# Four decay rows per head: picked by matmuls and a PSUM copy in place of eight small DMAs

## The chip, the cores and the metric

The kernel runs on one core of one Trainium2 chip. The metric is the device time of one execution in microseconds, as the median of several runs. TensorE (PE) multiplies, with its weight loads listed apart as PEld; VectorE (DVE), ScalarE (ACT) and GpSimd (POOL) do the elementwise work; SyncE (SP) and ScalarE issue the DMAs of this program. The kernel is written with tiles taken from pools; a scheduler orders the instructions of each engine when the program is built, and each engine runs its own list strictly in that order.

## The reference, cut to what matters

Causal attention with a decay term over four batches of eight heads (sequence 576, head size 64), then two dense layers of the same shape (512 to 2048 to 512) over the 2304 tokens:

```python
scores = (q @ k.T) / 8
cum    = cumsum(log(clip(f, 1e-4, 1)))
scores = where(causal, -1e9, scores + cum[:, None] - cum[None, :])
x      = softmax(scores) @ v                      # heads side by side: 2304 x 512
x      = relu(x @ w_in) ** 2 @ w_out              # first dense layer
out    = elu(x @ w_in2) @ w_out2                  # second dense layer
```

## The kernel before, in words

The decay is put into the score matmul. Below the 64 rows of transposed q and k, four more rows hold 8·cum and -8·cum, each as a rounded part and its remainder, against rows of ones. The contraction then runs over 68 rows and gives score plus decay in one product. All 32 heads' rows for their first 256 positions are made by `split_c` in the tile `ca`: head on the partition, the four rows along the free axis (4 x 512). A head needs them turned, as four partitions (64 to 67) of its operand tile `rawA`.

Batch 0 is handled in a special way. Its first 256 rows (kind "A", eight heads) come first, since they feed the first unit of the first dense layer; the rest of its rows (kinds "4" and "B") and the other batches follow. For kind "A", `fetch_plain` loads two heads into one `rawA` tile: rows 0 to 63 from `in_first_dram` and the values from `in_firstv_dram` on the SP queue, and the four decay rows from `ca` by one DMA per head, issued on ScalarE (the `nc.scalar.dma_start` of line 277).

While attention of batch 0 runs, the weights of the first dense layer are decoded. They come as 16 half tiles (`wraw`, `raws_w`), five of them fetched at the start. For each one ScalarE takes an absolute value (L153 in `words`), DVE does four steps (L154 to L157), ScalarE rounds to the high part `w` (L173), and GpSimd subtracts (L135) for the low part. The working tile of these steps is `wt`, with the pool tag `"o"` of pool `xa`, which has two buffers. The first five half tiles' decoding is spread over the first steps (`W_AT`). TensorE fills gaps with matmuls on a zero tile (`busy`, L250, tile `idle`): 60 at the start and a few per step.

Names in the rows: `s` scores in PSUM, `ea` the exponentials of kind "A", reduced by DVE (L354) and exponentiated by ScalarE (L357); `pt` their transposes, `pv` the product with the values, `xA` its copy, `pr` the turned row sums; `eb`, `pp` the same for kind "B"; `ph`, `o`, `pH`, `O`, `P` the dense layers. PSUM tiles `pt`, `pr` come from a pool of three banks (`ps_t`).

Of the kernel before, what the change touches and what calls it, by code (L numbers as in the profile page):

```python
# [10 lines left out]
F32 = mybir.dt.float32  # L11
F32R = mybir.dt.float32r
I32 = mybir.dt.int32
AF = mybir.ActivationFunctionType
ALU = mybir.AluOpType

B, H, S, D = 4, 8, 576, 64
# [25 lines left out]
PLAIN = (0,)  # L43
# [29 lines left out]
def f32(ap):  # L73
    return ap.bitcast(F32)
# [10 lines left out]
def attention_then_moe_kernel(ctx, tc, first, firstv, plain, qkv, aug0, f, w1, w2, out):  # L85
    nc = tc.nc
    PS = bass.MemoryType.PSUM

    def pool(stack, name, bufs, side, **kw):
        return stack.enter_context(tc.tile_pool(name=name, bufs=bufs, side=side, reuse_waits="tile", **kw))  # L90
# [5 lines left out]
    xa = pool(ctx, "xa", 2, "left")  # L96
# [27 lines left out]
    def copy(eng, dst, x, scale=None):  # L124
        if eng == "a":
            nc.scalar.activation(out=dst, in_=x, func=AF.Copy, scale=1.0 if scale is None else scale)  # L126
        elif eng == "p":
            nc.gpsimd.tensor_scalar(dst, x, 1.0 if scale is None else scale, 0.0, op0=ALU.mult, op1=ALU.add)
        elif scale is None:
            nc.vector.tensor_copy(dst, x)  # L130
        else:
            nc.vector.tensor_scalar(dst, x, scale, None, op0=ALU.mult)
# [65 lines left out]
    ps_t = pool(at, "ps_t", PSB[1], "right", space=PS)  # L198
# [14 lines left out]
    e4s = [a1.tile([128, 640], F32, name=f"e4_{s}") for s in range(2)]  # L213
    me = getattr(nc, MEM)
    ca = wa.tile([B * H, 4, 512], F32R, tag="w7", name="ca")
    me.memset(f32(ca), 1.0)
    nc.gpsimd.memset(mz, 0.0)
    mask(mz[:, 384:512], [[-1, 128]])
# [37 lines left out]
    pairs = {}  # L256
# [9 lines left out]
    def fetch_plain(b, h, part):  # L266
        g = b * H + h
        k = h % 2
        if part == "A":
            if k == 0:  # L270
                if h // 2 < BUFS["raw"]:
                    t = ab.tile([128, ALL], F32, tag="raw", name="rawA", bufs=BUFS["raw"])
                else:
                    t = hd.tile([128, RAW], F32, tag="qk1", name="rawA", bufs=BUFS["qs"])
                nc.sync.dma_start(out=t[0:64, 0:1024], in_=first[h // 2])
                for i in range(2):
                    nc.scalar.dma_start(out=t[64:68, 512 * i:512 * i + 512], in_=f32(ca[g + i:g + i + 1]))
                nc.sync.dma_start(out=t[:, 1024:1280], in_=firstv[h // 2])
                pairs[b, h // 2] = t
            t = pairs[b, h // 2]  # L280
            raws[b, h, part] = Plain(t, 512 * k - Q0, 512 * k + 256, t[:, 1024 + 128 * k:1152 + 128 * k].rearrange("p (j d) -> p j d", d=D))
            return
        if k == 0:
            t = ab.tile([128, ALL], F32, tag="raw", name="rawB", bufs=BUFS["raw"])
        else:
            t = hd.tile([128, RAW], F32, tag="qk1", name="rawC", bufs=BUFS["qs"])
        nc.sync.dma_start(out=t[0:64, 0:RAW], in_=plain[h])
        nc.sync.dma_start(out=t[64:68, 0:RAW], in_=aug[g])
        if k == 0:
            v = t[:, RAW:ALL]  # L290
        else:
            v = hd.tile([128, 5 * D], F32, tag="vv", name="vp", bufs=BUFS["vv"])
        nc.sync.dma_start(out=v, in_=qkv[b, h, :, RAW:ALL])
        raws[b, h, part] = Plain(t, 0, QW, v.rearrange("p (j d) -> p j d", d=D))

    def aug_split():
        cp, cn = (ab.tile([32, 2, S - 256], F32R, tag="eb", name=t, bufs=BUFS["eb"]) for t in ("cp", "cn"))
        split_c(cp, cn, slice(256, S))
        return cp, cn
# [53 lines left out]
    def reduce_min(e, s, m, nm, init=BIG):  # L353
        nc.vector.tensor_tensor_reduce(out=e, in0=s, in1=m, scale=-0.125, scalar=init, op0=ALU.add, op1=ALU.min, accum_out=nm)  # L354
# [15 lines left out]
    def soft_a(b, h, hh):  # L370
        e = ab.tile([128, 384], F32, tag="ea", name="ea", bufs=BUFS["ea"])
        nm = ab.tile([128, 2], F32, tag="nm2", name="nm2", bufs=3)
        z = sums("A", b, h // 2, h % 2)
        s = ps_s.tile([128, 512], F32, tag="s", name="s")
        scores(s[:, 0:256], hh, Q0 + 128, 0, 256, True, True)
        scores(s[:, 256:512], hh, Q0, 0, 256, True, True)
        parts = [slice(0, 256), slice(256, 384)]
        for i, c in enumerate(parts):
            n = c.stop - c.start
            reduce_min(e[:, c], s[:, c], mz[:, 512 - n:512], nm[:, i:i + 1])  # L380
            expo(e[:, c], nm[:, i:i + 1], z[:, i:i + 1])
        return e
# [156 lines left out]

    def soft(b, hp, kind, k):  # L540
        if kind == "A":
            es[b, hp, kind, k] = soft_a(b, 2 * hp + k, heads[b, hp, k])
            yield
        elif kind == "B":
            es[b, hp, kind, k] = yield from soft_b(b, 2 * hp + k, heads[b, hp, k])
        else:
            e4[b, hp] = soft_4(b, hp, [heads[b, hp, i] for i in range(2)])
            yield
# [180 lines left out]
    for i in range(len(todo) + LAG):  # L729
# [16 lines left out]
        if i < len(todo):  # L746
            sg = soft(*todo[i])
            b, hp, kind, k = todo[i]
        else:
            sg = iter(())  # L750
        if i >= LAG:
            o = todo[i - LAG]
            og = outs(*o)
        else:
            o, og = None, iter(())
# [416 lines left out]
```

## Time and profile before

| what | us |
|---|---|
| three timed runs | 1035.57, 1040.85, 1042.72 |
| their median | 1040.85 |
| the profiled execution, its own time | 1037.57 |
| span from its first to its last instruction | 1035.7 |
| TensorE busy in it | 1020.5 (99%) |
| VectorE busy in it | 683.1 (66%) |
| ScalarE busy in it | 547.4 (53%) |
| GpSimd busy in it | 275.0 (27%) |

Busy shares are averages over stages with different limits, so the table alone does not tell what bounds a stage. The mean granted TensorE clock of the whole execution is 0.994 of full speed.

### The profile page before, as it was taken

Reading aid. Unit: us, or ns where it says so; the run is one execution under the profiler, and the core shown is the slowest. Engines: PE = TensorE matmul, PEld = TensorE weight load, DVE = VectorE, ACT = ScalarE, POOL = GpSimd, SP = SyncE. Lnnn points to the kernel's source line nnn. Section 1 sums busy time; section 2 is a strip of 40 time slices with the busy share of each in tenths; the row PEclk is TensorE's granted clock in tenths of the full one; section 3 lists DMA queues with packets and bytes.
Section 4 is the critical chain, followed back from the end, with each engine's and each line's share of the span. In section 5 each row is a group of like instructions: output and inputs, shape, how many; then the busy total and the mean of one; then the engine's idle time right before and its main releaser. Section 6 shows DMA issues by size and latency. Waiting matters only on the chain.

```text
span 1035.7 us, 17605 instructions
## 1 busy us (share of the span) xinstructions
PE 1020.5 (99%) x6391; PEld 903.5 (87%) x6391; DVE 683.1 (66%) x1543; ACT 547.4 (53%) x1218; POOL 275.0 (27%) x296
## 2 busy tenths in 40 slices
PE   8999999999999999999999999999999999999998
PEld 7676798999999998889988888988988998899897
DVE  4995467665675638847385868896555989754554
ACT  3875688777786734524253535463344565433331
POOL 3565587675776210004103040300000000000000
PEclk8999999999999999999999999999999999999999
DMA  8853645554551164433454555544314465443502
GB/s 247 227 156 109 203 140 170 191 171 145 153 164 54 45 222 137 141 123 143 135 171 170 196 204 199 216 139 179 123 61 158 149 223 170 136 169 124 156 21 82
DMA packets 73881, 158.46 MB, mean 153 GB/s; under 512 B 9316, under 2 KB 34660, under 8 KB 73764
## 3 DMA queue, kind: packets, MB, share of 16 engines
q1 hardware_dynamic: 73732, 157.29, 46.4%
q8 instruction: 50, 0.82, 0.3%
q14 instruction: 35, 0.29, 0.1%
q10 hardware_dynamic: 64, 0.07, 0.0%
HBM read 115.15 MB, written 39.22 MB: 149 GB/s over the span
## 4 chain that ended last, share of the span: by engine, by line
PE 81%; DVE 9%; DMA 3%; POOL 2%; ACT 2%; issue 2%; POOLq 0%; ACTq 0%; DVEq 0%; SPq 0%
PE O L186 29%; PE P L186 16%; PE pH L186 11%; PE o L186 6%; PE ph L186 5%; PE pt L418 4%; PE pv L425 3%; PE s L350 2%; DVE wt L156 2%; PE s L351 2%; PE s L346 1%; DMA x<-yl 1%; PE pv L422 1%; DVE wt L157 1%; POOL qk L135 1%
## 5 line engine op out<-in xcount | busy, mean ns | idle before, releaser
L186 PEld LDWEIGHTS P<-xu,v 128*128 128x128 f32 x1536 | 200.5, 189 | 10.7 <-ACT hs L1013 0.6
L186 PE MATMUL P<-xu,v 128*128 128x256 f32 x1536 | 203.7, 282 | 0.5 <-ACT hs L1013 0.5
L186 PE MATMUL O<-v,gh 128*128 128x512 f32 x576 | 169.2, 393 | 1.4 <-ACT gh L984 1.4
L186 PE MATMUL pH<-xu,w 128*128 128x512 f32 (+1 forms) x672 | 140.8, 360 | 0.0
L186 PEld LDWEIGHTS pH<-xu,w 128*128 128x128 f32 x672 | 114.0, 188 | 20.2
L186 PE MATMUL O<-gh,w 128*128 128x512 f32 (+1 forms) x448 | 122.6, 362 | 0.0
L186 PEld LDWEIGHTS O<-v,gh 128*128 128x128 f32 x576 | 102.8, 188 | 19.4 <-ACT gh L984 1.8
L186 PE MATMUL O<-v,gl 128*128 128x512 f32 x288 | 101.0, 393 | 0.0
L186 PEld LDWEIGHTS O<-gh,w 128*128 128x128 f32 x448 | 79.8, 189 | 14.1
L135 POOL TENSOR_TENSOR yl<-pr,yh 128x512 fp32r<-128x512 f32 x18 | 25.2, 1398 | 249.9 <-ACT yh L833 172.1
L1013 ACT ACTIVATE hs<-P 128x256 f32<-128x256 f32 x128 | 48.0, 381 | 79.5 <-PE P L186 78.8
L135 POOL TENSOR_TENSOR qk<-raw,qk 64x704 fp32r<-64x704 f32 (+1 forms) x48 | 75.7, 1578 | 21.0 <-ACT qk L126 15.7
L186 PE MATMUL O<-gl,w 128*128 128x512 f32 (+1 forms) x224 | 80.1, 363 | 0.0
L1016 DVE TENSOR_TENSOR hs<-P,hs 128x256 f32<-128x256 f32 x96 | 40.4, 422 | 57.9 <-PE P L186 56.0
L186 PE MATMUL o<-gh,w 128*128 128x256 f32 x384 | 75.3, 290 | 0.0
L1038 ACT ACTIVATE g<-g 128x512 f32<-128x512 f32 x64 | 40.2, 629 | 54.8 <-DVE g L1030 32.9
L186 PE MATMUL ph<-xu,w 128*128 128x256 f32 x480 | 67.5, 287 | 1.0 <-DMA xu<-x 0.8
L153 ACT ACTIVATE wt<-wraw 128x512 f32<-128x512 f32 x57 | 38.2, 671 | 55.8 <-DMA wraw<-in_w_dram 42.0
L587 ACT ACTIVATE gh<-g 128x512 fp32r<-128x512 f32 (+1 forms) x80 | 46.9, 586 | 39.3 <-DVE g L586 34.8
L984 ACT ACTIVATE gh<-g 128x512 fp32r<-128x512 f32 x72 | 45.4, 631 | 35.4 <-DVE g L1039 28.6
L586 DVE TENSOR_TENSOR g<-g 128x512 f32<-128x512 f32 (+1 forms) x56 | 45.4, 811 | 26.9 <-ACT g L582 26.7
L186 PEld LDWEIGHTS ph<-xu,w 128*128 128x128 f32 x480 | 60.8, 190 | 1.6 <-DMA xu<-x 1.1
(153 smaller groups left out, 2089.1 us busy)
## 6 DMA issues: line engine op xcount, KB each, us to landing
xu<-x SPq DMA_DIRECT2D x66, 512.0 KB
wraw<-in_w_dram SPq DMA_DIRECT2D x57, 512.0 KB
raw<-in_qkv_dram SPq DMA_DIRECT2D x24, 800.0 KB
x<-yh SPq DMA_DIRECT2D x31, 256.0 KB
x<-yl SPq DMA_DIRECT2D x31, 256.0 KB
x<-xs SPq DMA_DIRECT2D x16, 320.0 KB
xu<-x SPq DMA_DIRECT2D x16, 256.0 KB
raws_w<-in_w_dram SPq DMA_DIRECT2D x7, 512.0 KB
```

What stands on the lines that cost most here:

```text
L135: nc.gpsimd.tensor_tensor(out=dst, in0=x, in1=f32(hi), op=ALU.subtract)
L153: nc.scalar.activation(out=f32(t), in_=f32(hi), func=AF.Abs)
L156: nc.vector.scalar_tensor_tensor(t, hi, -0x40000000, t, op0=ALU.bitwise_and, op1=ALU.bitwise_or)
L186: nc.tensor.matmul(out=dst, lhsT=l, rhs=r, start=first and i == 0, stop=last and i == n - 1, skip_group_check=skip)
L418: seen[0] = nc.tensor.transpose(dst, src, ident[:, c0:c0 + 128])
L425: seen[0] = nc.tensor.matmul(out=dst, lhsT=hh[2][:, J, :], rhs=hl[i], start=first and i == 0, stop=last and i == 1)
L586: (nc.vector if sq == "v" else nc.gpsimd).tensor_tensor(out=g[:, 0:n], in0=g[:, 0:n], in1=g[:, 0:n], op=ALU.mult)
L587: nc.scalar.activation(out=gh[:, 0:n], in_=g[:, 0:n], func=AF.Copy)
L984: nc.scalar.activation(out=gh, in_=g, func=AF.Copy)
L1013: nc.scalar.activation(out=o, in_=x, func=AF.Copy)
L1016: nc.vector.tensor_tensor(o, y, x, op=ALU.add)
L1038: nc.scalar.activation(out=gs[i], in_=gs[i], func=AF.Exp)
```

## The change

Line 277's eight DMAs go away. In their place `pick_rows(h)` multiplies `ca` with a matrix that holds a single one. The tile `one` (32 x 160, zero but for a one at column 67 + 4p of partition p) is made once by GpSimd; a 128-column window of it, starting at column 4h + 3 - r, moves row r of head h to output partition 64 + r. Four such matmuls of 512 columns accumulate in one PSUM bank `pk`, and partitions 64 to 67 of it are copied to `rawA`, by VectorE for even heads and by ScalarE for odd ones. Heads 0 and 1 are picked before the scores of head 0, head h + 1 before those of head h. `one` is allocated under the tag `"o"`.

```diff
+    one = xa.tile([B * H, 160], F32R, tag="o", name="one")
+    nc.gpsimd.memset(f32(one), 0.0)
+    nc.gpsimd.affine_select(out=one, in_=f32(one), pattern=[[1, 160]], compare_op=ALU.not_equal, fill=1.0, base=-67, channel_multiplier=-4)
     me.memset(f32(ca), 1.0)
...
                 nc.sync.dma_start(out=t[0:64, 0:1024], in_=first[h // 2])
-                for i in range(2):
-                    nc.scalar.dma_start(out=t[64:68, 512 * i:512 * i + 512], in_=f32(ca[g + i:g + i + 1]))
                 nc.sync.dma_start(out=t[:, 1024:1280], in_=firstv[h // 2])
...
+    def pick_rows(h):
+
+        t, k = pairs[0, h // 2], h % 2
+        pk = ps_t.tile([128, 512], F32, tag="t", name="pk")
+        for r in range(4):
+            c = 4 * h + 3 - r
+            nc.tensor.matmul(out=pk, lhsT=one[:, c:c + 128], rhs=ca[:, r, :], start=r == 0, stop=r == 3)
+        copy("va"[k], t[64:68, 512 * k:512 * k + 512], pk[64:68, :])
...
         if kind == "A":
+            if b in PLAIN:
+                h = 2 * hp + k
+                for i in ([0, 1] if h == 0 else [h + 1] if h < H - 1 else []):
+                    pick_rows(i)
             es[b, hp, kind, k] = soft_a(b, 2 * hp + k, heads[b, hp, k])
```

The scheduler makes new lists from this. The lists differ in the work of batch 0 and agree after it. The text below speaks of three places in them. The first is ScalarE's list at the last two of the first six decay DMAs; `ea` and `zA` are the exponentials of a head and their sums. Before:

```order
L277 DMA rawA<-ca 4x1x512 [waits DMAHW2_49]
L277 DMA rawA<-ca 4x1x512 [waits DMAHW4_49]
L153 ACTIVATE wt<-raws_w 128x512 [waits DMAHW7_49]
L357 ACTIVATE ea,zA<-ea,nm_266 128x256 [waits DVE_49]
L357 ACTIVATE ea,zA<-ea,nm_266 128x128 [waits DVE_49]
L153 ACTIVATE wt<-raws_w 128x512
L277 DMA rawA<-ca 4x1x512 [waits DMAHW6_49]
```

ScalarE's list at the same place after the change (`pk` is the PSUM bank of a head's picked rows, `w_0` the first decoded weight tile):

```order
L228 ACTIVATE nm_149<-fr 32x1 [waits Activation_49]
L153 ACTIVATE wt<-raws_w 128x512 [waits DMAHW7_49]
L173 ACTIVATE w_0_254<-wt 128x512 [waits DVE_49]
L126 ACTIVATE rawA<-pk 4x512 [waits PE_49]
L153 ACTIVATE wt<-raws_w 128x512 [waits DMAHW0_49,Pool_49]
L369 ACTIVATE ea,zA<-ea,nm_277 128x256 [waits DVE_49]
```

The first half tile's absolute value now follows the logarithm's table work directly, where six DMA issues with waits stood, and the second half tile's has got a wait for GpSimd that it did not have.

The second place is VectorE's list where the first half tiles are decoded; before, behind the reduction of the second head's scores (`nm_289` is its minimum):

```order
L354 ISA ea,nm_289<-s,mz 128x128
L354 ISA nm_289 128x1
L154 TENSOR_SCALAR wt<-wt 128x512 [waits Activation_49]
L155 TENSOR_SCALAR wt<-wt 128x512 [waits DVE_49]
L156 SCALAR_TENSOR_TENSOR wt<-raws_w,wt 128x512 [waits DMAHW7_49,DVE_49]
L154 TENSOR_SCALAR wt<-wt 128x512 [waits Activation_49]
L157 SCALAR_TENSOR_TENSOR wt<-raws_w,wt 128x512 [waits DVE_49]
```

VectorE's list there after the change, where `cn` is the last of the split decay rows:

```order
L237 SCALAR_TENSOR_TENSOR cn<-cum,cn 32x320 [waits DVE_49]
L154 TENSOR_SCALAR wt<-wt 128x512 [waits Activation_49]
L155 TENSOR_SCALAR wt<-wt 128x512 [waits DVE_49]
L156 SCALAR_TENSOR_TENSOR wt<-raws_w,wt 128x512 [waits DMAHW7_49,DVE_49]
L157 SCALAR_TENSOR_TENSOR wt<-raws_w,wt 128x512 [waits DVE_49]
L130 COPY rawA<-pk 4x512 [waits PE_49] x2
L366 ISA ea,nm_277<-s,mz 128x256 [waits PE_49,Pool_49]
```

The whole decoding of the first half tile has moved ahead of the first two heads' reductions, and ahead of the copies of heads 0 and 2. Before, the second half tile's L154 ran between the first one's L156 and L157; now the four steps of each of the first five half tiles end before the next one's begin.

The third place is TensorE's list behind the filling matmuls of the start; before:

```order
L250 MATMUL idle<-zero 128x256 x59
L346 MATMUL s<-rawA 128x256 [waits DMAHW2_49,DMAHW1_49]
L346 MATMUL s<-rawA 128x256
L250 MATMUL idle<-zero 128x256 x3
L346 MATMUL s<-rawA 128x256 [waits DMAHW4_49]
```

TensorE's list there after the change, from the last eight of twelve picking matmuls (heads 0, 1 and 2) on, which follow the fillers:

```order
L305 MATMUL pk<-ca,one 128x512 x8
L358 MATMUL s<-rawA 128x256 [waits DMAHW1_49,DVE_49]
L358 MATMUL s<-rawA 128x256
L255 MATMUL idle<-zero 128x256 x3
L358 MATMUL s<-rawA 128x256 [waits Activation_49]
```

Picking matmuls have come between the fillers and the first scores, and head 0's scores wait for VectorE's copy, head 1's for ScalarE's, where both waited for decay DMAs.

## Rows read from the trace of the kernel before

**Rows 1.** Stretches: start:end, length; busy us of each engine (instructions); clock, DMA share, GB/s.

```profile
14.00:18.00 4.00, 4.00 (x14) 3.37 (x14) 2.25 (x11) 3.08 (x10) 0.06 (x1) 0.50 0.84 259
18.00:22.00 4.00, 4.00 (x15) 3.01 (x13) 2.49 (x6) 0.49 (x1) 1.37 (x2) 0.50 0.95 247
...
26.00:50.00 24.00, 22.71 (x129) 16.48 (x128) 23.41 (x61) 19.90 (x54) 14.47 (x15) 1.00 0.82 229
...
700.00:800.00 100.00, 100.00 (x620) 89.68 (x620) 52.56 (x102) 38.87 (x81) 0.00 (x0) 1.00 0.37 128
```

**Rows 2.** The critical chain, 7 to 27 us: start, length, what held it.

```profile
7.46 4.97 DMA rawA<-ca
...
12.56 1.37 PE s L346 x4
```

**Rows 3.** Who waited for whom, 9 to 27 us: total, times, longest.

```profile
ACT wt L153 <- DMA rawA<-ca: 8.8, 1, 8.8
DVE ea L354 <- PE s L346: 7.5, 2, 5.9
PE s L346 <- DMA rawA<-ca: 1.7, 1, 1.7
```

**Rows 4.** Timeline to 15 us: issues on SP and ACT, the first half tile.

```profile
10.83 0.55 SPq L731 DMA_DIRECT2D aug<-in_aug_dram  x1
...
14.45 0.66 ACT L153 ACTIVATE wt<-raws_w 128x512 f32<-128x512 f32 x1 [8.77 <-DMA rawA<-ca]
```

**Rows 5.** VectorE's timeline: the last decoding step of half tiles 1, 2 and 5.

```profile
18.75 0.68 DVE L157 SCALAR_TENSOR_TENSOR wt<-raws_w,wt 128x512 int32<-128x512 int32 x1
...
24.22 0.84 DVE L157 SCALAR_TENSOR_TENSOR wt<-raws_w,wt 128x512 int32<-128x512 int32 x1
...
36.59 0.69 DVE L157 SCALAR_TENSOR_TENSOR wt<-wraw,wt 128x512 int32<-128x512 int32 x1
```

**Rows 6.** Groups by line and shape, 10 to 90 us: busy, mean ns, idle before.

```profile
L135 POOL TENSOR_TENSOR w<-wt,w 128x512 fp32r<-128x512 f32 x16 | 21.5, 1344 | 20.5 <-ACT w L173 20.5
...
L173 ACT ACTIVATE w<-wt 128x512 fp32r<-128x512 f32 x16 | 10.1, 629 | 8.7 <-DVE wt L157 8.6
...
L153 ACT ACTIVATE wt<-wraw 128x512 f32<-128x512 f32 x9 | 6.1, 673 | 1.2 <-POOL w L135 1.1
...
L126 ACT ACTIVATE ea<-pt 128x384 f32<-128x384 f32 x8 | 3.9, 484 | 4.0 <-PE pt L418 3.9
...
L126 ACT ACTIVATE xA<-pv 64x256 f32<-64x256 f32 x8 | 3.0, 375 | 1.0 <-POOL x L135 0.5 <-PE pv L422 0.4
```

**Rows 7.** Timeline: a decoding on VectorE, free and beside GpSimd; copies from PSUM.

```profile
16.88 0.42 DVE L154 TENSOR_SCALAR wt<-wt 128x512 f32<-128x512 f32 x1
17.34 0.43 DVE L155 TENSOR_SCALAR wt<-wt 128x512 int32<-128x512 int32 x1
17.80 0.69 DVE L156 SCALAR_TENSOR_TENSOR wt<-raws_w,wt 128x512 int32<-128x512 int32 x1
...
30.59 1.47 POOL L135 TENSOR_TENSOR w<-wt,w 128x512 fp32r<-128x512 f32 x1
...
30.95 1.66 DVE L156 SCALAR_TENSOR_TENSOR wt<-wraw,wt 128x512 int32<-128x512 int32 x1
...
81.86 0.41 DVE L130 COPY pp<-pt 128x256 f32<-128x256 f32 x1
...
85.62 0.47 DVE L130 COPY pp<-pt 128x320 f32<-128x320 f32 x1
```

**Rows 8.** TensorE's timeline: twelve matmuls of 512 columns, and what follows.

```profile
406.01 2.98 PE L186 MATMUL pH<-xu,w 128*128 128x512 f32 x12
408.83 0.63 PE L186 MATMUL O<-gh,w 128*128 128x512 f32 x2
```

**Rows 9.** What TensorE waited for, 24 to 100 us: total, times, longest.

```profile
PE pv L422 <- DVE pp L130: 2.1, 1, 2.1
PE pr L418 <- POOL rb L128: 1.0, 1, 1.0
```

## The prediction

> **What bounds the kernel now.** I read first the stretches, to see which engine is full in which part of the execution, then the chain of waits and the list of waits around the decay DMAs, then the timeline there.
>
> From about 90 us to the end TensorE is the bound: 100.00 of 100 us busy in a late stretch [rows 1], and nearly as full in the others there. What happens early can move the end only by shifting the moment at which this stream begins to run freely. That moment is near 80 us: the one long wait of TensorE between 24 and 100 us, 2.1 us for VectorE's `pp` [rows 9]. Before it, from 26 us on, VectorE is full (23.41 of 24 us) and TensorE nearly so (22.71 of 24) [rows 1]. So two streams run side by side up to 80 us, and VectorE's arrives last by 2.1 us. Most of VectorE's work there is decoding half tiles of weights.
>
> The early part, up to 24 us, is another matter. The chain goes through the decay DMA of head 0, which takes 4.97 us to land, and then through TensorE's scores [rows 2]. TensorE waits 1.7 us for that DMA, and ScalarE, held by its DMA issues, waits 8.8 us before its first half tile [rows 3]: it starts that at 14.45 us, though the tile was there by 10.83 us, when SP issued the transfer that waits for it [rows 4]. From 14 to 22 us TensorE's granted clock is 0.50, its lower level of 1.2 GHz [rows 1]; what it did just before was to sit idle for those 1.7 us behind the fillers. VectorE waits 7.5 us for scores [rows 3].
>
> **The change part by part.** The eight DMAs move 8 KB each; their transfer is worth nothing, their place is. With them gone ScalarE is free at the logarithm's end.
>
> *First scores.* ScalarE's absolute value (0.67 us [rows 6]) starts at 10.83 and ends at 11.5. VectorE's four steps follow: 0.92 from the start of L154 to that of L156, and 0.69 for each of the last two [rows 5, 7], together 2.3, so 13.8. Only then comes the copy of head 0's rows, since it stands behind them in VectorE's list. A copy of 4 x 512 from PSUM is not in the trace. Its bounds are 0.41 for 256 columns and twice that; 320 columns take 0.47, so 64 columns cost 0.06, and I take 0.65 for 512 [rows 7]. The scores of head 0 then start at 14.5 us instead of 12.56 [rows 2]: 1.9 us later. The DMA wait is replaced by a wait for weights and for the copy behind them. ScalarE's copies, by its rows for 384 and 256 columns (0.484 and 0.375, so 0.11 for 128), take 0.59 each [rows 6].
>
> *Picking matmuls.* Twelve matmuls of 512 columns take 2.82 us from the first to the next group's start [rows 8], 0.235 each; that the contraction is over 32 rows rather than 128 no row prices, so 0.235 is taken, with nothing below it assumed. Twelve of the 32 fall into the gap after the fillers, which opens at 10.86 us (12.56 less 1.7), and fill it to 13.7; TensorE then waits 0.8 us rather than 1.7. The other 20 stand between scores and transposes of heads 3 to 7 and cost up to 4.7 us of TensorE's stream, since the number of fillers does not fall.
>
> *The clock.* At 0.50 from 14 to 22 us TensorE did in 8 us what takes 4 at full speed [rows 1]. With matmuls where the idle gap was, I take it that the clock holds, which gives back 4 us. The Trainium skill, "TensorE: Matmul & The Clock Gate", section "What's actually happening", says that the default state is throttled and activity releases the throttle. The rows agree in that the fall follows an idle gap. By that rule the picks keep the clock; by the remaining wait of 0.8 us they might not, and this is a rival below.
>
> *TensorE's stream up to 80 us* is then 1.9 later at its start, 4 shorter by the clock and 4.7 longer by the picks: +2.6 us. Against that it had waits of 2.1 and 1.0 us to give up on the way [rows 9]: -0.5 if both go, +0.5 if only the 2.1 does. I take the latter, since the 1.0 is for GpSimd's `rb`, and nothing in the change moves GpSimd's work on the row sums forward.
>
> *VectorE's stream.* Here the tile `one` matters. It holds one of the two buffers of tag `"o"` until the last pick, so the first five half tiles go through the other one. A half tile's absolute value must wait until GpSimd has finished the one before, as ScalarE's new wait shows. One round is then 0.67 on ScalarE, 2.3 on VectorE, 0.63 for the rounding and 1.34 for GpSimd's subtraction [rows 6], 4.9 us, with four hand-overs between engines some 5.1. That is the lower end: nothing else is ahead in any queue. Reductions of scores, their exponentials and the new copies stand in the same lists; with one copy of 0.65 on VectorE and one of 0.59 on ScalarE in the way, the round is 6.3. I take 5.8, nearer the upper end, because the lists put a head's whole softmax between the steps of nearly every half tile.
>
> The Trainium skill, "SBUF — State Buffer", has a rule on this: VectorE operations with two SBUF inputs and GpSimd share a port pair under an exclusive lock, and the loser waits. The trace agrees: L156 took 1.66 us while GpSimd's subtraction ran and 0.69 without [rows 7]. With one buffer a half tile's subtraction ends before the next one's steps begin, so the new round is reckoned with 0.69. By the blocked row it would be 1 us longer.
>
> Before, the fourth step L157 of half tile 1 ended at 19.43 us and that of the fifth at 37.28 [rows 5], a round of 4.46 us. After, the first ends at 13.8, the fifth at 13.8 + 4 x 5.8 = 37.0, with ends 34.2 and 39.0. So a lead of 5.6 us at the first half tile is spent by the fifth: -0.3 us, between -3.1 and +1.7. All four of VectorE's copies lie within these four rounds. From there the lists hold the same work, and a full VectorE hands its difference on to 80 us.
>
> *What costs nothing.* GpSimd's two instructions for `one` stand in its list of start-up settings, which ends before the fillers do; from 14 to 18 us GpSimd is busy for 0.06 us [rows 1]. SP's queue is freer, not fuller: the order of its later transfers moves, but TensorE waits for none of the loads of kind "B" [rows 9]. If that cover were gone, a wait for one load would be some 5 us, by the decay DMA's 4.97 [rows 2].
>
> **Sum.** The later of the two streams sets the end: VectorE -0.3, TensorE +0.5. I take +0.5 on the profiled execution's 1037.57 us (a span of 1035.7 and 1.9 around it), so 1038.1. That execution is 3.3 us below the median of the three runs, 1040.85, and 2.0 above the fastest; the mean of all four is 1039.2. I put the sum on that middle: the forecast is 1039.7 us, no change. A measurement of this kernel can tell about 1%, 10 us, from no change; its own runs spread over 7.2 us.
>
> **The rivals.**
>
> *The round is short.* Near 5.1 us, VectorE leads by 3.1 us at the fifth half tile. For it: ScalarE's 8.8 us and VectorE's 7.5 us of early waits are gone. Against it: TensorE's stream, which is +2.6 without waits and can give up 3.1 at most, so -0.5. A half-speed stretch somewhat longer than the 8 us of the rows would make that -1.5. On the mean of 1039.2 that is 1038.
>
> *The clock falls all the same, and the one buffer decides.* TensorE still waits 0.8 us for the copy behind the first half tile, and later for exponentials. With half speed as before, its stream is 1.9 + 4.7 = +6.6, less 3.1 of waits, +3.5 us. VectorE alone decides from a round of 5.87 us on ((37.28 - 13.8) / 4): at 6.3 it is 1.7 us late. This ends slower, by 2 to 4 us: 1043. For it: a wait on TensorE remains and the fillers are no more than before. Against it: 2.8 us of matmuls in the gap.
>
> *The start is hidden anyway.* If TensorE's pace after 24 us had more slack than its listed waits, both streams meet at 80 us as before, and the result is 1039. This cannot be told from the forecast by the time.
>
> *The lists of batch 0 bring a new stall.* The scheduler reorders kinds "4" and "B" up to about 110 us. A stall of 10 us would need more than any wait now in the rows.
>
> **How the numbers follow.** Forecast (with the hidden start) 0.62, short round 0.16, clock and buffer 0.18, a new stall 0.04. The scatter of single runs is -3.6 to +3.6 about their middle; the cases lie at 1038 to 1043. The range that leaves out 2 in 10 is 1034.5 to 1045. Faster by over 1% would take 10 us, and the early streams hold no more than 8.8 us of ScalarE's wait, of which TensorE's stream lets at most 1.5 through: 0.02. Slower by over 1%: 0.04. Within 1%: 0.94.
>
> **What would show it.** Right: the first scores near 14.5 us behind a copy `rawA<-pk`; L157 of the first half tile near 13.8 us; rounds of 5 to 6.3 us up to the fifth; ScalarE's absolute values waiting for GpSimd; granted clock 1.00 from 14 to 22 us; TensorE's wait near 80 us still there, within 2 us of its old place. Wrong: a granted clock of 0.50 in a stretch before 30 us; the fifth L157 before 34 or after 39 us; a wait of TensorE of more than 3 us between 24 and 120 us.

## The result, and the profile after

The changed kernel is slower, by 0.9%. Each median is over all runs of a kernel, taken on the same chip.

| | before | after |
|---|---|---|
| median, us | 1041.66 (11 runs, 1035.57 to 1044.1) | 1053.31 (11 runs, 1042.43 to 1056.44) |
| ratio, 95% interval | | 1.0094 [1.0069, 1.0119] |
| profiled execution, us | 1037.57, span 1035.7, mean clock 0.994 | 1053.33, span 1051.3, mean clock 0.990 |

The forecast was 1039.7 us with a range up to 1045.0. Each run also lists its mean granted clock. Eight of the eleven after runs show 0.985 to 0.992 and take 1050.24 to 1056.44 us; the other three show 0.998 and take 1042.43 to 1042.87 us.

The stretches of the profile after, with the columns of [rows 1] (window and length, busy us of TensorE, its weight loads, VectorE, ScalarE and GpSimd with their instructions, granted clock, DMA share, GB/s):

```profile
14.00:18.00 4.00, 4.00 (x12) 3.23 (x12) 2.10 (x7) 2.02 (x6) 1.18 (x1) 0.50 1.05 283
18.00:22.00 4.00, 4.00 (x12) 2.98 (x11) 2.12 (x7) 0.99 (x4) 0.90 (x2) 0.50 1.05 322
22.00:26.00 4.00, 4.00 (x15) 3.09 (x14) 0.00 (x0) 2.40 (x5) 1.27 (x1) 0.50 0.67 196
26.00:31.00 5.00, 5.00 (x18) 3.35 (x17) 2.10 (x7) 1.81 (x6) 0.00 (x0) 0.53 0.42 140
...
26.00:50.00 24.00, 24.00 (x120) 17.23 (x118) 15.33 (x42) 14.18 (x41) 7.47 (x9) 0.90 0.50 139
```

The clock is at its lower level of 1.2 GHz from 13.6 us not for the 10.2 us of the kernel before, but up to 30.7 us. VectorE has nothing to do from 22 to 26 us, and the two engines have changed places from 26 to 50 us: TensorE is full with 24.00 of 24 us, VectorE has 15.33, where it had 23.41 [rows 1].

The chain of what ended last, 9 to 42 us (start, length, what held it), is TensorE alone, while before it went through a decay DMA [rows 2]:

```profile
8.96 2.04 PE idle L255 x17
11.00 3.22 PE pk L305 x12
14.21 2.01 PE s L358 x4
16.22 0.64 PE idle L255 x3
16.86 1.71 PE s L358 x4
...
21.13 2.00 PE pk L305 x4
...
28.42 2.22 PE idle L255 x9
30.64 1.16 PE pk L305 x4
```

Fillers, picks and scores follow one another with no gap: the copy of head 0's rows ends at 13.8 us, and the first scores start when the picks end. Four scores take 1.71 us here at the lower level (four scores at the higher one take 0.86 from 38 us on), four picks take 2.00 us at 21 us and 1.16 at 30.6.

The list of waits, 9 to 50 us (who waited for whom, total, times, longest), answers to [rows 3]:

```profile
POOL w L135 <- ACT w L173: 24.0, 5, 9.1
DVE ea L366 <- PE pv L434: 9.5, 3, 7.7
...
ACT wt L153 <- DMA raws_w<-in_w_dram: 4.7, 1, 4.7
...
ACT rawA L126 <- PE pk L305: 3.1, 1, 3.1
```

ScalarE's wait of 8.8 us for the decay DMA is gone, as planned. In its place VectorE waits 7.7 us at a stretch behind TensorE, and GpSimd 24.0 us for the decode. The last decoding step of the first five half tiles on VectorE's timeline [rows 5], with the copy behind the first:

```profile
12.41 0.69 DVE L157 SCALAR_TENSOR_TENSOR wt<-raws_w,wt 128x512 int32<-128x512 int32 x1
13.13 0.69 DVE L130 COPY rawA<-pk 4x512 f32<-4x512 f32 x1
...
19.89 0.69 DVE L157 SCALAR_TENSOR_TENSOR wt<-raws_w,wt 128x512 int32<-128x512 int32 x1
...
32.55 0.69 DVE L157 SCALAR_TENSOR_TENSOR wt<-wraw,wt 128x512 int32<-128x512 int32 x1
...
39.38 0.69 DVE L157 SCALAR_TENSOR_TENSOR wt<-wraw,wt 128x512 int32<-128x512 int32 x1
...
46.12 0.69 DVE L157 SCALAR_TENSOR_TENSOR wt<-wraw,wt 128x512 int32<-128x512 int32 x1
```

The fifth ends at 46.8 us instead of 37.3 [rows 5]. From there the delay is handed on: the first `ph` matmul starts at 58.4 us instead of 48.8, the first `o` at 94.3 instead of 84.6, the first `O` at 401.5 instead of 388.9. So 9.6 us are lost before 59 us, and some 3 more by 107 us, where TensorE waits 2.2 us for ScalarE's copy `xB` and the clock falls a second time, for 3.4 us from 98.9. A last 3 us fall behind 401 us, in small waits of TensorE whose order differs; they weren't studied.

### The profile page after: what moved, and what is told of

It is laid out like the page before. It is cut to its first block, busy times and chain, and to the rows that moved or that the text cites. A ratio compares the mean times of both kernels' runs of the same rounds, so it can differ in the third digit from the quotient of the medians.

```text
span 1051.3 us, 17674 instructions
## 1 busy us (share of the span) xinstructions
PE 1035.0 (98%) x6423; PEld 912.8 (87%) x6423; DVE 688.0 (65%) x1547; ACT 550.2 (52%) x1222; POOL 272.7 (26%) x298
## 4 chain that ended last, share of the span: by engine, by line
PE 83%; DVE 9%; DMA 3%; ACT 2%; issue 2%; POOL 1%; SPq 0%; ACTq 0%; POOLq 0%; DVEq 0%
PE O L186 28%; PE P L186 15%; PE pH L186 11%; PE o L186 6%; PE ph L186 5%; PE pt L430 4%; PE pv L437 3%; PE s L363 2%; PE s L362 2%; PE s L358 2%; PE idle L255 2%; DVE wt L156 2%; PE pv L434 1%; DMA x<-yl 1%; DVE wt L157 1%
## 5 line engine op out<-in xcount | busy, mean ns | idle before, releaser
L186 PEld LDWEIGHTS P<-xu,v 128*128 128x128 f32 x1536 | 200.6, 189 | 13.1 <-DMA xu<-x 1.2
L135 POOL TENSOR_TENSOR yl<-pr,yh 128x512 fp32r<-128x512 f32 x18 | 24.8, 1380 | 252.3 <-ACT yh L849 175.2
L1054 ACT ACTIVATE g<-g 128x512 f32<-128x512 f32 x64 | 40.2, 628 | 54.2 <-DVE g L1046 32.3
L603 ACT ACTIVATE gh<-g 128x512 fp32r<-128x512 f32 (+1 forms) x80 | 46.8, 586 | 38.7 <-DVE g L602 35.7
L1000 ACT ACTIVATE gh<-g 128x512 fp32r<-128x512 f32 x72 | 45.4, 631 | 34.4 <-DVE g L1055 27.6
L186 PEld LDWEIGHTS o<-gh,w 128*128 128x128 f32 x384 | 60.4, 191 | 1.7 <-issue 1.6
```

The source lines that it names most:

```text
L135: nc.gpsimd.tensor_tensor(out=dst, in0=x, in1=f32(hi), op=ALU.subtract)
L186: nc.tensor.matmul(out=dst, lhsT=l, rhs=r, start=first and i == 0, stop=last and i == n - 1, skip_group_check=skip)
L603: nc.scalar.activation(out=gh[:, 0:n], in_=g[:, 0:n], func=AF.Copy)
L1000: nc.scalar.activation(out=gh, in_=g, func=AF.Copy)
L1054: nc.scalar.activation(out=gs[i], in_=gs[i], func=AF.Exp)
```

## The experiments

Theories: **the clock** (matmuls over 32 rows don't keep TensorE's clock up), **one buffer** (the table `one` leaves the decode a single buffer), **the picks' time** (32 more matmuls on TensorE), and **the copies** (eight copies out of PSUM on VectorE and ScalarE, and scores that wait for them). In each table below, "against before" is the ratio to the kernel before, which ran beside it on the same chip, with its 95% interval. "Half speed" is worked out from a run's mean clock, 2 x (1 - clock) x span, and averaged over the runs. Over the 29 runs of the kernel before that went with the first four experiments, each us at half speed goes with 0.40 us of time (a straight line through them).

### One buffer or the clock: four kernels

*Own buffer.* The table goes into a tile that is empty until batch 1.

```diff
-    one = xa.tile([B * H, 160], F32R, tag="o", name="one")
+    one = ptA[1][1][0:B * H, 0:160]
```

> The changed kernel, with the table of ones in a part of a tile that stands empty until batch 1 and not in one of the two buffers that the weight decode rotates through. If the single buffer for the decode makes the loss (rounds of 6.7 to 12.6 us between the first five half tiles): the fifth result of the decode stands at 34 to 39 us and not at 46.8, the first 128x256 product of the first weight (ph) starts near 49 to 51 us and not at 58.4, and the time is 1040 to 1044 us. If the clock makes it: the granted clock is again 0.50 from about 13.6 to 30 us, the decode is quicker by less than 4 us at the fifth result, since VectorE's and ScalarE's work before it waits for TensorE, and the time is 1048 to 1054 us. If the picks' own place among the matmuls makes it: 1048 to 1054 us too.

*Full rows.* The picks contract over 128 rows. The order of instructions is the changed kernel's on every engine.

```diff
-    ca = wa.tile([B * H, 4, 512], F32R, tag="w7", name="ca")
+    caf = wa.tile([128, 4, 512], F32R, tag="w7", name="ca")
+    ca = caf[0:B * H]
-    one = xa.tile([B * H, 160], F32R, tag="o", name="one")
+    one = xa.tile([128, 160], F32R, tag="o", name="one")
-    me.memset(f32(ca), 1.0)
+    me.memset(f32(caf), 1.0)
...
-    nc.tensor.matmul(out=pk, lhsT=one[:, c:c + 128], rhs=ca[:, r, :], start=r == 0, stop=r == 3)
+    nc.tensor.matmul(out=pk, lhsT=one[:, c:c + 128], rhs=caf[:, r, :], start=r == 0, stop=r == 3)
```

> The changed kernel in the same order of instructions on every engine, with the picks contracting over 128 rows and not over 32 (the other 96 rows of the table of ones are zero), so they are as long and only fill more of the array. If the clock falls because matmuls over 32 rows don't hold it: the granted clock stays at 1.00 from 7 us on (or falls for less than 4 us), the first ph starts at 49 to 53 us and not at 58.4, and the time is 1040 to 1045 us. If the single buffer makes the loss: the rounds of the decode are still 6 us and more, and the time stays at 1048 to 1054 us whatever the clock does. If the fall has nothing to do with the rows: the clock is 0.50 from about 13.6 us for about 17 us as before this edit, 1050 to 1054 us.

*Full rows and own buffer.* Both edits together.

> Both edits: picks over 128 rows, and the table of ones outside the decode's two buffers. By the clock alone: as with the full rows alone, 1040 to 1045 us. By the buffer alone: as with the own buffer alone, 1040 to 1044 us. If both have a part: 3 us or more below the better of the two single edits, 1036 to 1041 us. If neither has, and the picks among the matmuls cost the time: 1048 us or more.

*One buffer in the kernel before.* The table alone, held by one small matmul a head.

```diff
+    one = xa.tile([B * H, 160], F32R, tag="o", name="one")
+    nc.gpsimd.memset(f32(one), 0.0)
+    nc.gpsimd.affine_select(out=one, in_=f32(one), pattern=[[1, 160]], compare_op=ALU.not_equal, fill=1.0, base=-67, channel_multiplier=-4)
...
+                for i in ([0, 1] if h == 0 else [h + 1] if h < H - 1 else []):
+                    nc.tensor.matmul(out=idle[:, 0:32], lhsT=one[:, 4 * i:4 * i + 128], rhs=one[:, 0:32], start=True, stop=True)
```

> The kernel before with its DMAs, and a table of ones that holds one of the two buffers of the weight decode until head 7 (one 128x32 matmul a head reads it, and its result is used nowhere). It has no picks and no copies. By the clock: 0.50 for about 10 us as in the kernel before [rows 1], and 1040 to 1045 us, the decode a little later. By the single buffer: rounds of over 6 us, the fifth result of the decode at 43 us or later and not at 37.3 [rows 5], and 1048 to 1054 us.

| | median, us (runs) | against before | mean clock of the runs | fifth L157 ends | first ph |
|---|---|---|---|---|---|
| after | 1053.31 (11) | 1.0094 [1.0069, 1.0119] | 0.985 to 0.998 | 46.8 | 58.4 |
| own buffer | 1051.54 (6) | 1.0090 [1.0056, 1.0125] | 0.984 to 0.993 | 35.1 | 58.3 |
| full rows | 1042.88 (12) | 1.0019 [1.0006, 1.0033] | 0.995 to 1.000 | 43.3 | 54.8 |
| full rows, own buffer | 1040.44 (12) | 0.9999 [0.9983, 1.0014] | 0.993 to 1.000 | 30.8 | 52.8 |
| before, one buffer | 1044.14 (12) | 1.0030 [1.0007, 1.0053] | 0.987 to 0.998 | 47.4 | 50.0 |

The buffer alone gives back nothing that can be told from zero: the fifth half tile comes 11.7 us sooner, and the first `ph` at the same time. The rows alone bring the median down by 10.4 us (7.8 by the ratios). Once they do, the buffer is worth 2.4 more, and in the kernel before, where it delays the fifth half tile by 10.2 us, it costs 0.3%. So one buffer was dear for the decode and cheap for the end, since TensorE and not VectorE decided there. Against the expectations: own buffer has the time and the clock of the clock theory, but its fifth half tile gained more than the 4 us at most that this theory allowed; full rows has the time, but its first `ph` is later than 53 us and its profiled clock still falls; the kernel before with one buffer has the slow rounds of the buffer theory and a time that the clock theory forecast.

TensorE's timeline after (start, length, engine, line, operation with its shape, and in brackets the idle time before it and what ended it):

```profile
8.80 2.20 PE L255 MATMUL idle<-zero 128*128 128x256 f32 x17
10.93 3.29 PE L305 MATMUL pk<-ca,one 32*128 32x512 f32 x12
14.14 2.08 PE L358 MATMUL s<-rawA 68*128 68x256 f32 x4
```

The same timeline of the kernel with full rows:

```profile
9.25 0.89 PE L255 MATMUL idle<-zero 128*128 128x256 f32 x6
9.97 2.95 PE L305 MATMUL pk<-ca,one 128*128 128x512 f32 x12
15.01 1.22 PE L358 MATMUL s<-rawA 68*128 68x256 f32 x2 [2.09 <-DVE rawA L130]
```

With 32 rows the clock fell at 13.59 us, inside the picks, though TensorE had not been idle since the fillers began. With full rows it held through the picks and fell at 15.01 us, behind 2.09 us in which TensorE waited for the copy, and for 10.2 us, not 17.1. This profiled run was the slowest of its twelve (1045.29 us); on the mean the runs with full rows are at half speed for 4.2 us, those of after for 19.3, and with the own buffer it is 7.6 against 26.9. At 0.40 us for each of these, the clock accounts for 6.1 of the 8.1 us between the means of after and full rows, and for 7.7 of 9.2 with the own buffer (an estimate); the 32 rows have a second cost beside it, the longer picks below.

### Rows, without copies and without waits

*DMAs kept, picks unread.* Full rows and own buffer, but the eight DMAs are back and the copies are out: the kernel before, plus 32 picks that nobody reads.

```diff
+                for i in range(2):
+                    nc.scalar.dma_start(out=t[64:68, 512 * i:512 * i + 512], in_=f32(ca[g + i:g + i + 1]))
...
-        copy("va"[k], t[64:68, 512 * k:512 * k + 512], pk[64:68, :])
```

> full_rows_own_buffer with the DMAs of the decay rows put back and the copies left out: the 32 picks go to PSUM and are read by nobody. It is the kernel before plus 32 picks. If the picks' time on TensorE lies beside other work: 1038 to 1041 us, like the kernel before. If it is on the path once the clock is held: the picks behind the first scores (20 of 0.235 us, 4.7 us) push the first ph from 48.8 to 52 to 54 us, and the time is 1041 to 1044 us. In the gap from 10.86 to 12.56 us [rows 2] the first 12 picks need 2.8 us, so the first scores come at 13.5 to 14 us.

*The same over 32 rows.* In the same order on every engine.

```diff
-            nc.tensor.matmul(out=pk, lhsT=one[:, c:c + 128], rhs=caf[:, r, :], start=r == 0, stop=r == 3)
+            nc.tensor.matmul(out=pk, lhsT=one[0:B * H, c:c + 128], rhs=ca[:, r, :], start=r == 0, stop=r == 3)
```

> dmas_kept_picks_unused in the same order on every engine, with the unread picks over 32 rows and not over 128. Nothing waits for the picks in either, no buffer is held, no copy is made: only the rows differ. If matmuls over 32 rows don't hold the clock: 0.50 from about 13.5 us for 10 us or more, where the kernel with full rows stayed at 1.00 up to 675 us, and the time is 1043 to 1050 us. If the rows don't matter and only idle time does: 1035 to 1038 us, the clock at 1.00.

*Fillers over 32 rows.* The kernel before, its 60 fillers over 32 rows of zeros.

```diff
-    busy(WARM)
+    for _ in range(WARM):
+        nc.tensor.matmul(out=idle[:, 0:256].rearrange("p (a b) -> p a b", a=2), lhsT=zero[0:32], rhs=zero[0:32].unsqueeze(1).broadcast_to([32, 2, 128]), start=True, stop=True)
```

> The kernel before with its 60 fillers ahead of the first scores contracting over 32 rows of zeros and not over 128. If 32-row matmuls don't raise the clock: 0.50 from the start to 20 us or later, each filler takes about 0.21 us in place of 0.107, they end near 13.5 us and not at 10.7, and the time is 1043 to 1052 us. If the rows don't matter: the clock is 1.00 from about 6.5 us as in the kernel before [rows 1], and 1040 to 1042 us.

| | median, us (runs) | against before | mean clock of the runs |
|---|---|---|---|
| DMAs kept, picks unread, full rows | 1035.84 (12) | 0.9954 [0.9937, 0.9970] | 0.997 to 1.000 |
| the same, 32 rows | 1038.36 (12) | 0.9995 [0.9968, 1.0022] | 0.998 to 1.000 in nine, 0.990 to 0.992 in three |
| fillers over 32 rows | 1044.11 (10) | 1.0029 [1.0010, 1.0048] | not comparable |

The first is the fastest kernel here, below everything that was expected of it (1038 to 1044 us). Its stretches, with the columns as above, are these:

```profile
14.00:18.00 4.00, 4.00 (x25) 3.46 (x23) 3.36 (x14) 3.12 (x10) 0.00 (x0) 1.00 0.70 222
18.00:22.00 4.00, 4.00 (x28) 3.30 (x27) 2.31 (x8) 3.35 (x10) 3.18 (x4) 1.00 0.64 140
```

TensorE gets through 28 matmuls from 18 to 22 us where before it got through 15 [rows 1], and the clock holds from 6.4 us to 675 us. The 7.5 us of picks cost nothing that shows. The runs of before that went beside this kernel average 1040.9 us with 13.7 us at half speed, and 0.37 us for each of them; brought to this kernel's 1.0 us that is 1036.2, and it took 1036.1 on average.

With 32 rows in the same places the profiled run held its clock and took 1038.28 us. Its first twelve picks, and below them those over 128 rows:

```profile
10.66 3.06 PE L307 MATMUL pk<-ca,ptA 32*128 32x512 f32 x12
13.64 1.13 PE L359 MATMUL s<-rawA 68*128 68x256 f32 x4
```

```profile
10.66 2.97 PE L307 MATMUL pk<-ca,ptA 128*128 128x512 f32 x12
13.46 1.03 PE L359 MATMUL s<-rawA 68*128 68x256 f32 x4
```

The picks over 32 rows are a little longer, and the nine runs with the clock at 0.998 or more average 1038.3 us, 2.2 above the mean over 128 rows. By these nine it looks as if the rows did nothing to the clock; but three of twelve runs fell to 0.990 to 0.992 and took 1046.05 to 1048.06 us, as none of the twelve with full rows did. The expected 1043 to 1050 us hold for these three alone. So 32 rows make a fall possible, not certain, and in after and own buffer, where the scores wait for a copy behind the picks, 14 of 17 runs show 0.993 or less, against 2 of 24 of their twins with full rows. What decides between two runs of one program was not found.

The fillers show it best. TensorE's timeline in the kernel before:

```profile
1.05 9.81 PE L250 MATMUL idle<-zero 128*128 128x256 f32 x60 [1.05 <-DVE zero L245]
```

And with the fillers over 32 rows:

```profile
1.05 13.16 PE L253 MATMUL idle<-zero 32*128 32x256 f32 x60 [1.05 <-DVE zero L245]
14.15 2.08 PE L347 MATMUL s<-rawA 68*128 68x256 f32 x4
15.66 1.20 PE L250 MATMUL idle<-zero 128*128 128x256 f32 x3
16.66 1.91 PE L347 MATMUL s<-rawA 68*128 68x256 f32 x4
```

Sixty matmuls back to back took 0.22 us each, all at the lower level, and four scores after them 1.91 us, their length at 0.50. The records of the clock begin in every trace with its first rise; that comes at 6.4 us before and at 29.35 us here, behind full-row fillers and transposes. (So the mean clock of these runs leaves the start out.) The Trainium skill, "TensorE: Matmul & The Clock Gate", section "What's actually happening", says that the clock is set by how busy TensorE has been recently. By its own timeline TensorE was busy for 13 us without a gap here, and the clock stayed low: if busy means that a matmul runs, the page and the measurement differ, and the measurement decides.

### How many picks, and the gap behind the fillers

*Eight picks.* The ones in the table stand 32 columns apart, so four picks bring the rows of four heads; once over full rows, once over 32, both with the buffer of their own.

```diff
-    nc.gpsimd.affine_select(out=one, in_=f32(one), pattern=[[1, 160]], compare_op=ALU.not_equal, fill=1.0, base=-67, channel_multiplier=-4)
+    nc.gpsimd.affine_select(out=one, in_=f32(one), pattern=[[1, 259]], compare_op=ALU.not_equal, fill=1.0, base=-3, channel_multiplier=-32)
...
-            c = 4 * h + 3 - r
+            c = 128 * q + 3 - r
...
-        copy("va"[k], t[64:68, 512 * k:512 * k + 512], pk[64:68, :])
+        for i in range(4):
+            k = i % 2
+            copy("va"[k], pairs[0, 2 * q + i // 2][64:68, 512 * k:512 * k + 512], pk[32 * i:32 * i + 4, :])
```

> As full_rows_own_buffer, but four picks serve four heads: the ones in the table stand 32 columns apart, so that the rows of heads 0 to 3 come out on rows 0, 32, 64 and 96 of one PSUM tile, and 8 picks do the work of 32. The copies are the same eight. If the picks' time among the matmuls still costs something: 24 picks of 0.235 us [rows 8] are 5.6 us less on TensorE, of which those behind the first four lie on the chain of full_rows_own_buffer that is TensorE alone up to about 49 us, so the first ph comes 3 to 5 us sooner than its 52.8, and the time is 1036 to 1039 us. If they are hidden beside the weight decode: 1039 to 1042 us. If the fillers that the picks displaced come back and the clock falls for longer (4 picks leave an idle gap ahead of the scores as in the kernel before): half the speed for 10 us, and 1040 to 1043 us.

> The same 8 picks, contracting over 32 rows, own buffer. If it is the amount of 32-row work that lets the clock fall for 17 us: 8 picks take 1.9 us and not 7.5, so the clock is at half speed for 7 to 10 us, as in the kernel before, and the time is within 3 us of the same kernel with full rows, 1037 to 1043 us. If any 32-row matmul at the start does as much harm as 32 of them: half speed for about 17 us, and 1046 to 1052 us.

*More fillers ahead of the scores* in the kernel before.

```diff
-WARM, FILL, FILL_TO = 60, 2, 14
+WARM, FILL, FILL_TO = 78, 2, 14
```

> The kernel before with 78 in place of 60 fillers ahead of the first scores, so that TensorE works on zeros through the gap from 10.86 to 12.56 us in which it waits for the rows of decay; nothing else. If the idle gap makes the clock fall: the granted clock stays at 1.00 through 14 to 26 us, or is 0.50 for 7 us at most, and the time is 1036 to 1039 us, 2 to 4 us less than before. If the fall comes from what runs behind the gap (scores over 68 rows with fillers between): 0.50 for 10 us as before, only later, and 1039 to 1042 us.

*More fillers throughout* the first steps of the kernel before.

```diff
-WARM, FILL, FILL_TO = 60, 2, 14
+WARM, FILL, FILL_TO = 74, 5, 14
```

> The kernel before with 74 in place of 60 fillers ahead of the first scores and 5 (6 on the first step of a pair) in place of 2 (3) behind each of the first steps, no picks, no table, no copies. If what made dmas_kept_picks_unused 5 us faster than before was the clock held by full-row work and nothing else of the picks: the clock at 1.00 through 7 to 31 us and 1035 to 1038 us. If fillers behind every step cost TensorE's time on the path, since there are more of them than the 32 picks: 1039 us or more with the clock at 1.00.

| | median, us (runs) | against before | mean clock of the runs | first ph |
|---|---|---|---|---|
| eight picks, full rows | 1042.20 (12) | 1.0007 [0.9991, 1.0023] | 0.993 to 0.997 | 53.5 |
| eight picks, 32 rows | 1042.34 (12) | 1.0014 [0.9996, 1.0032] | 0.991 to 0.995 | 54.2 |
| 78 fillers ahead | 1038.89 (12) | 0.9986 [0.9966, 1.0006] | 0.995 to 1.000 | 45.4 |
| 74 ahead, 5 in place of 2 behind steps | 1045.93 (11) | 1.0053 [1.0036, 1.0069] | 0.997 to 1.000 | 54.1 |

Fewer picks gave no gain: with four in place of twelve ahead of the scores, TensorE stands idle again behind them, for 4.03 us over 128 rows and 4.39 over 32, and the clock falls in both kernels for 13.7 us of the profiled run. The first scores over 128 rows:

```profile
14.86 2.08 PE L359 MATMUL s<-rawA 68*128 68x256 f32 x4 [4.03 <-DVE rawA L130]
```

What the array did in the 1.1 us before, over 32 rows or 128, makes no difference. So eight 32-row picks don't do the harm of 32; whether so few do any, this pair can't tell, since the gap is there in both.

Filling the gap of the kernel before with full-row work holds the clock in the early stretches and lowers half speed from 13.7 to 5.0 us; the 2.4 us that come of it are within what the runs can tell from nothing. With 89 more fillers, some 10.7 us of TensorE at 0.12 each, the clock holds too, and 5.6 us are lost. That TensorE's time is on the path here was one of the two expectations, and the time (1039 us or more) agrees with it; but it isn't shown, for from 26 to 50 us it is VectorE that is nearly full (third in the row, behind TensorE and its weight loads):

```profile
26.00:50.00 24.00, 22.36 (x142) 17.71 (x141) 23.50 (x48) 16.43 (x42) 12.63 (x14) 1.00 0.94 258
```

The scheduler makes new lists for each of these kernels. Why 32 picks of 7.5 us went by for nothing when these fillers didn't was not settled.

### The copies

*Fillers in the gap* of full rows and own buffer, which the scheduler put among the first picks.

```diff
                     pick_rows(i)
+                busy(16 if h == 0 else 0)
```

> full_rows_own_buffer with 16 fillers among the first picks, where TensorE stood idle for 1.8 to 2 us until VectorE had copied the rows of head 0 out of PSUM behind its weight decode. If what is left of the loss is the clock after that gap: 1.00 through 14 to 26 us and 1035 to 1038 us, like dmas_kept_picks_unused. If it is the copies on VectorE and ScalarE and the scores that wait for them: the clock holds, and the time stays at 1039 to 1041 us.

*All copies on ScalarE.*

```diff
-        copy("va"[k], t[64:68, 512 * k:512 * k + 512], pk[64:68, :])
+        copy("aa"[k], t[64:68, 512 * k:512 * k + 512], pk[64:68, :])
```

> full_rows_own_buffer with all eight copies on ScalarE, none on VectorE, where the first waited behind the decode of the first half tile and half of the second. If VectorE is what the first scores wait for: they start before 14.5 us and not at 15.2, the idle gap is under 1.5 us, and the time is 1037 to 1040 us. If ScalarE's abs and rounding steps of the decode take VectorE's place ahead of the copies, or the decode starves behind four more copies of 0.59 us: 1040 to 1043 us.

*Copies that nobody waits for.* DMAs kept and picks over full rows, and the copies go to a tile that stands empty.

```diff
+        copy("va"[k], e4s[1][64:68, 0:512], pk[64:68, :])
```

> dmas_kept_picks_unused with the eight copies as well, out of PSUM into a tile that stands empty, four on VectorE and four on ScalarE: the DMAs bring the rows that the scores read, and nothing waits for the copies' results. If the loss of 4.6 us from dmas_kept_picks_unused (1035.8) to full_rows_own_buffer (1040.4) is the copies' own time on VectorE and ScalarE (0.69 and 0.59 us each): 1039 to 1041 us. If it is the scores of each head waiting for its copy behind the weight decode: 1035 to 1037 us.

| | median, us (runs) | against before | mean clock of the runs |
|---|---|---|---|
| fillers in the gap | 1045.78 (12) | 1.0057 [1.0035, 1.0079] | 0.991 to 0.998 |
| copies on ScalarE | 1039.84 (12) | 0.9987 [0.9972, 1.0003] | 0.997 to 1.000 |
| copies unread, DMAs kept | 1038.98 (12) | 0.9984 [0.9968, 1.0000] | 0.996 to 1.000 |

The copies' own work, with the new lists that it brings, costs some 3 us (ratio 0.9984 against 0.9954, intervals that touch). The scores' wait for them, with the DMAs gone, costs 1.6 us more (0.9999), which these intervals can't tell from nothing. With all copies on ScalarE the first scores start at 13.4 us, not 15.2, and the clock holds through the whole profiled run; by the ratios the time is 1.2 us less, which the intervals can't tell from nothing.

Fillers in the gap missed both expectations. Their clock is 0.996 or more in ten of twelve runs, and they are 5 us slower than without. VectorE's timeline shows copies that stand behind a decode:

```profile
14.42 0.69 DVE L130 COPY rawA<-pk 4x512 f32<-4x512 f32 x1
15.14 1.54 DVE L156 SCALAR_TENSOR_TENSOR wt<-raws_w,wt 128x512 int32<-128x512 int32 x1
16.71 0.69 DVE L157 SCALAR_TENSOR_TENSOR wt<-raws_w,wt 128x512 int32<-128x512 int32 x1
17.32 0.42 DVE L154 TENSOR_SCALAR wt<-wt 128x512 f32<-128x512 f32 x1
17.77 0.69 DVE L130 COPY rawA<-pk 4x512 f32<-4x512 f32 x1
18.49 1.20 DVE L155 TENSOR_SCALAR wt<-wt 128x512 int32<-128x512 int32 x1
19.72 0.42 DVE L366 CUSTOM_DVE_ANT_0 ea<-s,mz 128x256 f32<-128x256 f32 x1
```

The first reduction of scores comes at 19.72 us, behind two half tiles and two copies. Without the fillers it comes at 18.16 us, and in the kernel with the DMAs kept at 14.64 us:

```profile
18.16 0.42 DVE L366 CUSTOM_DVE_ANT_0 ea<-s,mz 128x256 f32<-128x256 f32 x1
```

```profile
14.64 0.42 DVE L367 CUSTOM_DVE_ANT_0 ea<-s,mz 128x256 f32<-128x256 f32 x1 [6.60 <-PE s L359]
```

So holding the clock is not enough. ScalarE's early start, which the change buys, lets the decode run ahead of the softmax on VectorE. That is argued from the order and the timeline; no kernel here held the decode back. Nor does it explain the 5 us: against the kernel without the fillers the first `pv` is 0.5 us later (25.3 against 24.8 us) and the last 4.3 us (56.3 against 52.0), so most is lost later, and its cause stays open.

### The sum of the loss

By the ratios to the kernel before, on its 1041 us: picks over full rows with the DMAs kept, -4.8 us (the clock held); the copies' work, +3.1; the scores waiting for them, +1.6; the one buffer, +2.1; 32 rows in place of 128, +7.8. Together +9.8, the measured ratio of 1.0094. (The medians are 11.65 us apart, since eight of eleven runs lie high; by medians the rows' term is 9.5.) These are steps along one path of kernels, so they add up by construction; each is uncertain by 2 us or more, in all but the last the lists change too, and on another path the steps are others: with the own buffer the rows are worth 9.5 (1.0090 against 0.9999), and without copies 4.3 (0.9995 against 0.9954).

## Why the prediction was wrong

**The step that failed** is *The clock*: "With matmuls where the idle gap was, I take it that the clock holds, which gives back 4 us." The matmuls were there, 12 in a row with no gap, and the clock fell within them, for 17.1 us. The step took a busy TensorE for what counts, and left the contraction over 32 rows out of it, though the prediction had noted under *Picking matmuls* that no row prices it. The full rows, with every engine's order unchanged, bring the ratio from 1.0094 to 1.0019. The size of 4 us was sound: the kernel that holds the clock over full rows, with the DMAs kept, is 4.8 us faster than before.

**The rival that came nearest** had the clock fall, but for another reason and at too small a price. "The clock falls all the same, and the one buffer decides" put the fall down to the waits left on TensorE, 0.8 us of them ahead of the first scores; the clock fell within the picks, with no wait before it. It gave 1043 us, because it took half speed as long as before. Half speed was 6.8 us longer at the start and came back for 3.4 us at 98.9; and not the buffer decided but TensorE.

**First scores, right in time, partly by luck.** At 14.14 us, forecast 14.5; the first L157 ended at 13.1, forecast 13.8. The copies took 0.69 on VectorE and 0.59 on ScalarE, forecast 0.65 and 0.59. But the forecast had TensorE wait 0.8 us for the copy; the copy was done at 13.8 us, and the chain goes through the picks, which took 3.22 us and not 2.82. Over full rows the wait is there, 2.09 us of it.

**Picking matmuls, right in size over full rows** (12 from 10.66 to 13.46 us with the DMAs kept, 0.233 each, forecast 0.235), a little short over 32: four of them take 1.11 us up to the next start and not 0.93. That the other 20 cost up to 4.7 us of TensorE was a bound; the kernel with the DMAs kept shows none of it.

**The round, too short.** Forecast 5.8 us and the fifth L157 at 37.0 (34.2 to 39.0); measured 7.5, 12.7, 6.8 and 6.7, and the fifth at 46.8. With full rows the rounds are still 7.2, 9.5, 6.2 and 6.2: the range of 5.1 to 6.3 priced a copy on each engine, but no wait of a head's softmax for TensorE, which stands in the same lists and took up to 7.7 us at a stretch. What a slow round costs was overrated in turn: a fifth half tile that is 10 to 12.5 us later cost 2.1 to 3.1 us at the end (1.0019 against 0.9999, and 1.0030).

**VectorE as the engine that decides, wrong.** Its -0.3 us rested on a full VectorE that hands its difference on. After, TensorE is full from 26 to 50 us and VectorE isn't. Where the clock holds, the eight copies cost some 3 us at the end, about what the four of 0.65 us on VectorE come to.

**What would show it** named the right rows: a granted clock of 0.50 before 30 us, and the fifth L157 after 39 us. The third sign, a wait of TensorE of over 3 us, didn't come: between 24 and 110 us the longest was 2.2 us.

## What to carry to other kernels

Before a few shallow matmuls replace something else at a start or in a gap, look at how many rows they contract over: padding the operands with zero rows to the full 128 cost no time here, and brought the runs with a mean clock of 0.993 or less from 14 of 17 down to 2 of 24. Useless full-row matmuls in a gap can be worth more than the work that a change removes: the kernel that kept all eight DMAs and ran the picks unread was the fastest, 0.5% below before. They aren't free everywhere: 89 more fillers in the same stretches held the clock and lost 5.6 us. And when a scheduler orders by estimated times, a transfer that leaves an engine's queue also moves everything that waited behind it; ask which engine's list it now runs ahead in.

## What the hardware showed that was not expected

- Sixty matmuls over 32 rows, back to back from 1.05 to 14.15 us, never raised TensorE's clock; sixty over 128 rows raised it by 6.4 us.
- A matmul over 32 rows was not quicker than one over 128 but slower, 0.28 us against 0.23 for 512 columns at the higher level (four of them, 1.11 and 0.93 us to the next start; twelve in a row, 0.25 and 0.23).
- The granted clock differs between executions of one program: the changed kernel's means run from 0.985 to 0.998, and its times follow them. A profile of one execution shows one of these.
